# Values loaded by head onto 96 partitions, the first queries split off, and a new instruction order, in an attention and MLP kernel

## The chip, the cores and the metric

The kernel runs on one core of a Trainium2 chip. The core has TensorE (matrix products, PE in the profile; its weight loads are PEld), VectorE (DVE), ScalarE (ACT), GpSimd (POOL) and SyncE (SP). Each takes its own queue of instructions in order, and they meet through semaphores. Transfers between DRAM and the on-chip memory (SBUF, 128 partitions) run on 16 DMA engines. The metric is the device time of one execution in microseconds (us).

## The reference

Four batches of four heads, 1088 tokens each, head width 32. Attention is linear, over products of two sketches; its output goes through a layer with h - tanh(h).

```python
def phi(x):                                    # S1, S2: 8 x 32
    a = np.einsum('rd,bhsd->bhsr', S1, x)
    b = np.einsum('rd,bhsd->bhsr', S2, x)
    return np.einsum('bhsi,bhsj->bhsij', a, b).reshape(*x.shape[:-1], 64)
q_p, k_p = phi(q), phi(k)
kv = np.einsum('bhsf,bhsd->bhfd', k_p, v)
z = np.sum(k_p, axis=2)
num = np.einsum('bhsf,bhfd->bhsd', q_p, kv)
den = np.einsum('bhsf,bhf->bhs', q_p, z)[..., None] + 1e-06
x = (num / den)                                # as 4352 tokens x 128
h = x @ w_in                                   # 128 x 2048
out = (h - np.tanh(h)) @ w_out                 # 2048 x 128
```

## The kernel before

The program is a list of operations, each with an engine, what it reads and what it writes. A table, ORDER, gives each engine its queue by the operations' numbers, in the sequence in which they are created; a negative number n stands for -n dummy products on TensorE. Waits are derived from reads and writes. An operation at the head of its queue that waits holds everything behind it on that engine.

**Loads.** All large loads are issued by SP: load_k, load_v, load_q, load_w_in and load_w_out. Tokens of a batch are numbered 34 j + c with j from 0 to 31. Keys and queries of a batch come as 128 partitions (head, j) with 1088 numbers each (544 KB), batch 0's keys in two parts. Values sit in vx with 32 c + j as the partition, where c is one of four groups of 9, 9, 9 and 7 tokens; load_v issues one load for each group, onto 32 partitions, with all four heads (L432 to L439). A rule in load (L405) lets a load be issued only when the one that lies about 1.9 MB before it in the list has landed. Key, query and value buffers alternate between batches. Values are read by the products called sums; queries go through a transpose on VectorE (q_transpose, qT, L608), as keys do (kT, L567 and L710).

**Start.** Batch 0's keys are projected (kproj0), transposed (kab0), their products made (wk) and summed with the values (sums0). The first 256 queries have a path of their own (first_factors, first_numerators): qab, qd, qpd, qpdT; fold0 and the small copy swc0 (L726) on ScalarE, then qc, cd, dd, dden, drec, rT; then num0 and x0, which writes the first 256 tokens of xT. Weights are cast to bf16: w_in on ScalarE (casts, L819), w_out on GpSimd (L823).

**The layer.** Tokens are taken in groups: 128, 128, 256, then 512 at a time, 256 last. For a group, first_layer makes 16 blocks of h (L887) with a tanh on ScalarE after each 512 columns (L892); second_layer adds w_out products (L906) and a linear part (lin, L932) into one PSUM bank, which VectorE copies out (o, tile osb, L947) before the next group may start there; SP then stores it (L954). The linear part needs the product of the two weight matrices, kept as whi (ScalarE) and wlo (VectorE, L863). In the text h2, o1, lin0 and the like mean these operations of group 2, 1 and 0, and o#0 the copy out of group 0. The last group is stored with one DMA (L942):

```python
out=ob[B - 1, :, 26:34, :].rearrange("j (c z) e -> c j (z e)", z=2), in_=osb[u][:, 0:256]
```

**Later batches.** For batch b: key transpose kT, kproj, kab, gram, fold, wk on GpSimd, sums; query transpose qT, qproj, qf (L631), dt, den, rec, an, qp on GpSimd (L660), qpT, num (L680), and the casts into xT (L690).

Of the kernel before, what the change touches and what calls it, by code (L numbers as in the profile page):

```python
# [10 lines left out]
B, H, S, D = 4, 4, 1088, 32  # L11
# [5 lines left out]
OFF = (0, 9, 18, 27)  # L17
NT = 9
# [2 lines left out]

ORDER = {
    "tensor": (
# [17 lines left out]
    ),  # L41
    "scalar": (
# [9 lines left out]
    ),  # L52
    "vector": (
# [4 lines left out]
    ),  # L58
    "gpsimd": (
        21, 3, 22, 9, 7, 10, 8, 4, 23, 75, 82, 84, 59, 60, 134, 61, 62, 132, 150, 149, 151, 277, 302, 300, 280, 281,  # L60
        283, 285, 301, 431, 454, 456, 434, 435, 437, 439, 455, 579, 582, 583, 585, 587,
    ),
    "sync": (
# [4 lines left out]
    ),  # L68
}

# [256 lines left out]
def bass_polysketch_attn__then__act_tanh_shrink_kernel(nc, q, k, v, S1, S2, moe_w_in, moe_w_out, out):  # L327
# [28 lines left out]
    qraw = [sb(f"qraw{i}", [128, S]) for i in range(2)]  # L356
    kT = [sb(f"kT{i}", [128, 4 * NT * 32]) for i in range(2)]
    qT = [sb(f"qT{i}", [128, S]) for i in range(2)]
    vx = [sb(f"vx{i}", [128, H, NT, D]) for i in range(2)]
# [45 lines left out]
    def load(eng, key, sem, due, fn, nbytes, also=False, rate=300, name="load"):  # L405

        o = P.op(eng, nbytes / rate, fn, w=() if also else key if isinstance(key, list) else [key], sem=sem, due=due,
                 name=name)
        if also:
            P.also(o, key)  # L410
        if eng == "sync":
            ahead = nbytes
            for x, n in reversed(flow):
                ahead += n
                if ahead > AHEAD:
                    o.deps.add(x)
                    break
            flow.append((o, nbytes))
# [6 lines left out]
    def load_k(b, due):  # L425
        cuts = ((0, 512), (512, S)) if b == 0 else ((0, S),)
        for x, (lo, hi) in enumerate(cuts):
            load("sync", [("kraw", b % 2, y) for y in ((x,) if b == 0 else (0, 1))], f"k{b}{x}", due, lambda e, lo=lo, hi=hi: e.dma_start(  # L428
                out=kraw[b % 2][:, lo:hi], in_=k[b].rearrange("h (j c) d -> (h j) (c d)", j=32)[:, lo:hi]),
                512 * (hi - lo), rate=400 if b == 0 else 300, name=f"load k{b}")  # L430

    def load_v(b, due):  # L432
        src = v[b].rearrange("h (j c) d -> j h c d", j=32)
        for c in range(4):
            n = NT if c < 3 else 7
            load("sync", ("vx", b % 2), f"v{b}{c}", due + c, lambda e, c=c, n=n: e.dma_start(
                out=vx[b % 2][32 * c:32 * c + 32, :, 0:n, :].rearrange("j h t d -> j h (t d)"),
                in_=src[:, :, OFF[c]:OFF[c] + n, :].rearrange("j h t d -> j h (t d)")),
                128 * 128 * n, True, 226, name=f"load v{b}")  # L439

    def load_q(b, due):
        i = b % 2
        load("sync", ("qraw", i), f"q{b}", due, lambda e: e.dma_start(
            out=qraw[i][:, :], in_=q[b].rearrange("h (j c) d -> (h j) (c d)", j=32)), 512 * S, name=f"load q{b}")

    def load_w_in(x, due):
        load("sync", ("w_in_f", x), f"wi{x}", due, lambda e: e.dma_start(
            out=w_in_f[:, 512 * x:512 * x + 512], in_=moe_w_in[:, 512 * x:512 * x + 512]), 262144, rate=390, name="load w_in")

    def load_w_out(x, due):  # L450
        load("sync", ("w_out_f", x), f"wo{x}", due, lambda e: e.dma_start(
            out=w_out_f[:, 4 * x:4 * x + 4, :].rearrange("p z c -> p (z c)"),
            in_=moe_w_out[512 * x:512 * x + 512, :].rearrange("(ji z) c -> ji (z c)", z=4)), 262144, rate=390, name="load w_out")
# [152 lines left out]
    def q_transpose(b, part, lo, hi):  # L606
        i = b % 2
        P.op("vector", dve(hi - lo), lambda e: e.transpose(out=qT[i][:, lo:hi], in_=qraw[i][:, lo:hi]),  # L608
             r=[("qraw", i)], w=[("qT", i, y) for y in (range(2) if part is None else (part,))], name="qT")

    def layout(nblk):
        nb = (nblk + 3) // 4
# [347 lines left out]
    constants()  # L960
    load_s()
    load_k(0, 100)
    load_q(0, 150)
    load_v(0, 200)
    load_w_in(0, 400)
    load_w_in(1, 450)
    load_w_in(2, 500)
    load_w_in(3, 550)
    load_w_out(0, 650)
    load_w_out(1, 700)  # L970
    load_k(1, 750)
# [77 lines left out]
```

## Time and profile before

| | us |
|---|---|
| median of 3 runs | 110.84 |
| lowest and highest | 109.92, 111.91 |
| the profiled execution | 111.44 |
| its span in the profile | 109.7 |
| TensorE busy in it | 101.0 |
| ScalarE busy | 84.4 |
| VectorE busy | 46.5 |
| GpSimd busy | 41.8 |

The profile shows one execution. Its page gives each engine's busy time, the span in 40 equal slices with busy tenths, and the chain of work that ended last, followed back from the end. A row of a timeline reads: start, length, engine, line, operation, tile written and tile read, form, count, and in brackets how long the engine stood idle before and what released it. A row of a table of stretches reads: from and to, length, busy time and count of each engine, the granted TensorE clock, the mean busy share of the 16 DMA engines (counts can take it a little over 1), and GB/s. Matmuls overlap in the pipeline, so a busy TensorE is not TensorE at its peak. The granted clock was 0.998.

### The profile page before, as it was taken

What the parts mean: (1) busy time and instruction counts of PE and PEld (TensorE: products, weight loads), DVE (VectorE), ACT (ScalarE), POOL (GpSimd) and SP (SyncE); (2) the same over time, 40 slices, a digit from 0 to 9 for tenths busy, and PEclk for the clock granted to TensorE, in tenths of its full rate; (3) what the DMA queues carried; (4) which work ended last, traced back from release to release, by engine and by line L of the source; (5) the groups of instructions that cost most, each with busy time, mean ns of one, the idle gap of its engine ahead of it and who ended that gap; (6) DMA issues with size and microseconds to landing.
All of it is one profiled execution on the core that took longest, in us unless ns stands there. A gap on an engine that the chain in (4) does not pass through costs nothing.

```text
span 109.7 us, 3290 instructions
## 1 busy us (share of the span) xinstructions
PE 101.0 (92%) x1406; PEld 57.4 (52%) x1406; DVE 46.5 (42%) x88; ACT 84.4 (77%) x184; POOL 41.8 (38%) x46
## 2 busy tenths in 40 slices
PE   5999998898988989999999999999999999999940
PEld 4956677574646734443546543454444444345730
DVE  2737999736859384075017402527600200200210
ACT  3132479765964769798998979999979999999920
POOL 5204435799117998004999500269300000000000
PEclk9999999999999999999999999999999999999999
DMA  2999999996766821023000500410023041032061
GB/s 68 311 234 233 298 324 284 210 318 127 235 219 195 216 47 21 6 37 59 6 0 6 92 7 0 75 26 0 0 46 49 7 75 21 0 57 42 6 96 48
DMA packets 22195, 11.24 MB, mean 102 GB/s; under 512 B 17828, under 2 KB 20004, under 8 KB 22180
## 3 DMA queue, kind: packets, MB, share of 16 engines
q1 hardware_dynamic: 22100, 11.02, 40.9%
q8 instruction: 11, 0.18, 0.8%
q14 instruction: 4, 0.03, 0.1%
q10 hardware_dynamic: 80, 0.01, 0.1%
HBM read 8.79 MB, written 2.23 MB: 100 GB/s over the span
## 4 chain that ended last, share of the span: by engine, by line
PE 46%; DMA 32%; ACT 14%; DVE 2%; SPq 1%; issue 1%; DVEq 0%
PE ps L887 17%; PE ps L906 16%; DMA qraw<-in_q_dram 16%; ACT tt L892 13%; DMA w_out_f<-in_moe_w_out_dram 7%; DMA kraw<-in_k_dram 6%; PE ps L680 4%; DMA w_in_f<-in_moe_w_in_dram 4%; PE ps L932 2%; PE ps L585 2%; PE ps L913 1%; PE ps L624 1%; DVE qT L608 1%; ACT xT L690 1%; SPq L428 1%; PE ps L538 1%
## 5 line engine op out<-in xcount | busy, mean ns | idle before, releaser
L892 ACT ACTIVATE tt<-ps 128x512 bf16<-128x512 f32 x136 | 70.3, 659 | 4.8 <-PE ps L887 4.4
L887 PE MATMUL ps<-xT,w_in 128*128 128x512 bf16 (+2 forms) x176 | 48.1, 335 | 1.3 <-ACT w_inT L849 0.5
L906 PE MATMUL ps<-tt,w_out 128*128 128x512 bf16 (+2 forms) x160 | 41.3, 337 | 0.0
L887 PEld LDWEIGHTS ps<-xT,w_in 128*128 128x128 bf16 x176 | 17.5, 114 | 21.5 <-ACT tt L892 10.6
L947 DVE STREAM_TRANSPOSE osb<-ps 128x512 f32<-128x512 f32 (+2 forms) x10 | 5.9, 587 | 32.5 <-PE ps L906 32.5
L906 PEld LDWEIGHTS ps<-tt,w_out 128*128 128x128 bf16 x160 | 14.6, 99 | 9.1 <-ACT tt L892 0.7
L558 POOL TENSOR_TENSOR wk<-kab 128x768 f32<-128x768 f32 x10 | 15.1, 1508 | 8.9 <-DVE kab L530 8.3
L660 POOL TENSOR_TENSOR qp<-an,qf 128x768 f32<-128x768 f32 (+1 forms) x11 | 16.2, 1470 | 2.1 <-DVE an L651 1.3
L665 DVE STREAM_TRANSPOSE qpT<-qp 128x768 f32<-128x768 f32 (+1 forms) x12 | 11.1, 927 | 10.8 <-POOL qp L660 10.7
L637 POOL TENSOR_TENSOR dt<-qf 128x288 f32<-128x288 f32 x3 | 2.4, 796 | 16.8 <-DVE qf L631 16.8
L1020 PE MATMUL ps<-wz 128*128 128x128 bf16 x81 | 8.2, 256 | 0.0
L1020 PEld LDWEIGHTS ps<-wz 128*128 128x128 bf16 x81 | 6.4, 117 | 2.9 <-issue 2.6
L690 ACT CAST xT<-ps 128x256 bf16<-128x256 f32 (+3 forms) x16 | 5.3, 391 | 2.9 <-PE ps L680 2.9
L608 DVE STREAM_TRANSPOSE qT<-qraw 128x1088 f32<-128x1088 f32 (+2 forms) x5 | 5.4, 1072 | 3.0 <-DMA qraw<-in_q_dram 3.0
L680 PE MATMUL ps<-qpT,ndw 32*32 32x288 f32 (+1 forms) x256 | 6.2, 399 | 0.0
L631 DVE STREAM_TRANSPOSE qf<-ps 128x1152 f32<-128x1152 f32 (+1 forms) x4 | 5.2, 1307 | 0.8 <-PE ps L624 0.8
L567 DVE STREAM_TRANSPOSE kT<-kraw 128x1088 f32<-128x1088 f32 x3 | 3.9, 1297 | 2.1 <-DMA kraw<-in_k_dram 2.1
L680 PEld LDWEIGHTS ps<-qpT,ndw 32*32 32x32 f32 x256 | 3.2, 103 | 2.1 <-DVE qpT L665 0.6
L585 PEld LDWEIGHTS ps<-wk,vx 128*32 128x32 f32 x216 | 3.2, 110 | 1.9 <-issue 1.1
L530 DVE STREAM_TRANSPOSE kab<-ps 128x576 f32<-128x576 f32 (+2 forms) x5 | 3.1, 645 | 2.4 <-PE ps L522 2.4
L585 PE MATMUL ps<-wk,vx 128*32 128x64 f32 x216 | 4.1, 221 | 0.0
L538 PE MATMUL ps<-kab 128*64 128x32 f32 x72 | 3.1, 225 | 0.9 <-DVE kab L530 0.9
(97 smaller groups left out, 78.0 us busy)
## 6 DMA issues: line engine op xcount, KB each, us to landing
qraw<-in_q_dram SPq DMA_DIRECT2D x4, 544.0 KB, 5.9
vx<-in_v_dram SPq DMA_DIRECT2D x12, 144.0 KB, 6.7
kraw<-in_k_dram SPq DMA_DIRECT2D x3, 544.0 KB, 6.0
w_in_f<-in_moe_w_in_dram SPq DMA_DIRECT2D x4, 256.0 KB, 6.0
w_out_f<-in_moe_w_out_dram SPq DMA_DIRECT2D x4, 256.0 KB, 6.3
out_dram<-osb SPq DMA_DIRECT2D x16, 64.0 KB, 2.0
vx<-in_v_dram SPq DMA_DIRECT2D x4, 112.0 KB, 6.0
kraw<-in_k_dram SPq DMA_DIRECT2D x1, 288.0 KB, 3.2
```

The costliest lines, as they stand in the source:

```text
L558: P.op(eng, dve(64 * n) if eng == "vector" else pool(64 * n), lambda e: e.tensor_tensor(out=wk[i][:, t0:t1, :, :, :].rearrange("p t h i j ...
L585: ins = e.matmul(su[32 * h:32 * h + 32, 0:64], vx[b % 2][:, h, t, :], wk[i][:, t, h, :, :], start=(t == 0), stop=(t == NT - 1), tile_posit ...
L608: P.op("vector", dve(hi - lo), lambda e: e.transpose(out=qT[i][:, lo:hi], in_=qraw[i][:, lo:hi]), r=[("qraw", i)], w=[("qT", i, y) for y i ...
L660: e.tensor_tensor(out=qp[u][:, 4 * lo:4 * hi, :, :], in0=(pa if head else an[u][:, 4 * lo:4 * hi, :])[:, :, :, None].to_broadcast([128, m, ...
L665: P.op("vector", dve(64 * m), lambda e, lo=lo, hi=hi: e.transpose(out=qpT[u][:, :, 32 * lo:32 * hi].rearrange("p x (n j) -> p x n j", j=32 ...
L680: ins = e.matmul(ps[32 * h:32 * h + 32, c, 0:N], ndw[i][32 * c:32 * c + 32, y, 32 * h:32 * h + 32], qpT[u][32 * c:32 * c + 32, 2 * h + y, ...
L690: P.op("scalar", act(cols), lambda e: e.copy(dst, src), r=bank[c[0]:c[1]], w=[("x", (lo + 32 * first) // 32 + t) for t in range(cols // 32 ...
L887: ins = e.matmul(bk[:, n * y:n * y + n], w_tile(jb), xT[:, t0:t0 + n], start=True, stop=True)
L892: P.op("scalar", act(512), lambda e, ts=ts, bk=bk: e.activation(out=tt[:, ts, :], in_=bk, func=AF.Tanh, scale=-1.0), r=[kb], w=[("t", ts)] ...
L906: ins = e.matmul(acc[:, 0:n], w_out[:, jb, :], tt[:, ts, n * y:n * y + n], start=o.start and y == 0, stop=o.stop and y == per - 1)
L947: P.op("vector", dve(n), lambda e: e.transpose(out=osb[u][:, 0:n], in_=acc[:, 0:n]), r=[ka], w=[("osb", u, 0), ("osb", u, 1)], due=when(t0 ...
L1020: P.emit(lambda e: e.matmul(ps[:, 6, 0:128], wz[:, 0:128], wz[:, 0:128], start=True, stop=True))
```

## The change

Values are loaded one head at a time onto 96 partitions (groups 0 to 2), with a fifth load for group 3. Batch 0's queries are split into the first 256 columns, issued behind the keys, and the rest, issued behind w_in. The planner's rates are other numbers (they do not enter the program once ORDER is given). ORDER is replaced.

```diff
     def load_v(b, due):
-        src = v[b].rearrange("h (j c) d -> j h c d", j=32)
-        for c in range(4):
-            n = NT if c < 3 else 7
-            load("sync", ("vx", b % 2), f"v{b}{c}", due + c, lambda e, c=c, n=n: e.dma_start(
-                out=vx[b % 2][32 * c:32 * c + 32, :, 0:n, :].rearrange("j h t d -> j h (t d)"),
-                in_=src[:, :, OFF[c]:OFF[c] + n, :].rearrange("j h t d -> j h (t d)")),
-                128 * 128 * n, True, 226, name=f"load v{b}")
+        src = v[b].rearrange("h (j x) d -> h j x d", j=32)
+        for h in range(H):
+            load("sync", ("vx", b % 2), f"v{b}{h}", due + h, lambda e, h=h: e.dma_start(
+                out=vx[b % 2][0:96, h, :, :].rearrange("p t d -> p (t d)"),
+                in_=src[h, :, 0:27, :].rearrange("j (c t) d -> c j (t d)", c=3)),
+                96 * 1152, True, 370, name=f"load v{b}")
+        load("sync", ("vx", b % 2), f"v{b}4", due + 4, lambda e: e.dma_start(
+            out=vx[b % 2][96:128, :, 0:7, :].rearrange("j h t d -> j h (t d)"),
+            in_=src[:, :, 27:34, :].rearrange("h j t d -> j h (t d)")),
+            128 * 896, True, 300, name=f"load v{b}")
...
+    def load_q(b, due, part=None):
         i = b % 2
+        lo, hi = ((0, S), (0, 256), (256, S))[0 if part is None else part + 1]
+        load("sync", [("qraw", i, y) for y in (range(2) if part is None else (part,))], f"q{b}{part}", due, lambda e: e.dma_start(
+            out=qraw[i][:, lo:hi], in_=q[b].rearrange("h (j c) d -> (h j) (c d)", j=32)[:, lo:hi]), 512 * (hi - lo), rate=380,
...
     load_k(0, 100)
-    load_q(0, 150)
+    load_q(0, 150, 0)
     load_v(0, 200)
...
     load_w_in(3, 550)
+    load_q(0, 600, 1)
     load_w_out(0, 650)
```

q_transpose now reads the part of qraw that it transposes. With five new loads ahead of them, later operations have numbers 3 to 5 higher. Put back into names, ORDER differs in these places that matter here (b1, b2, b3 are the batches; qT(0) is the first 256 queries, qT(0') the rest):

| engine | before | after |
|---|---|---|
| SP, first loads | k0, q0, v0, w_in, w_out, k1, w_out, v1, q1, k2, v2, k3, q2, stores, q3, v3 among stores | k0, q0 first part, v0, w_in, q0 rest, w_out, k1, w_out, v1, q1, k2, v2, q2, k3, q3, 12 stores, v3 |
| ScalarE | ..., zs0, swc0, cast w_in, cast w_in, kvb x4, cast w_in, cast w_in, ndw0, tanh | ..., zs0, s2blk, cast w_in, swc0, cast w_in x3, kvb x4, tanh |
| VectorE, start | sbd, kab0, kab0, qT(0), wk, wk, qd, qT(0'), wk, cd, ..., kvd, drec, qf(0), rT, dt, x0, den, rT, rec, x0 | sbd, qT(0), kab0, kab0, qd, wk, wk, wk, qpdT, cd, ..., kvd, dden, qT(0'), drec, rT, rT, x0, qf(0), x0 |
| VectorE, later | ..., kab(b1), qpT, wlo, qT(b1), kT(b2), o#0, qf(b1), kT(b3), kab(b2), den, qT(b2), rec, o#1, ndw, qT(b3), o#2 | ..., kab(b1), qpT x3, kT(b2), wlo, qT(b1), qT(b2), o#0, qf(b1), kT(b3), o#1, qT(b3), kab(b2), den, rec, o#2 |
| GpSimd | wk, qpd x2, cast w_out x2, qp, cast w_out x2, qp | wk, qpd x2, cast w_out x4, qp, qp |
| TensorE | ..., kproj0, s2rep, gram0, qab, fold0, qc, sums0 x4, qproj, num0, spread, h0; ... num, lin0, h2 and qproj(b1), o1 | ..., kproj0, s2rep, qab, gram0, fold0, one sums0, qc, three sums0, num0, qproj, h0, spread; ... num, lin0, h2 and qproj(b1), o1 |

TensorE's dummy products go from 81 to 68.

More of the change, by code (lines that the diff above doesn't have):

```diff
@@ L23 @@
     "tensor": (
[17 rows of a table removed]
[17 rows of a table added]
     ),
     "scalar": (
[9 rows of a table removed]
[9 rows of a table added]
     ),
     "vector": (
[4 rows of a table removed]
[4 rows of a table added]
     ),
     "gpsimd": (
-        21, 3, 22, 9, 7, 10, 8, 4, 23, 75, 82, 84, 59, 60, 134, 61, 62, 132, 150, 149, 151, 277, 302, 300, 280, 281,
-        283, 285, 301, 431, 454, 456, 434, 435, 437, 439, 455, 579, 582, 583, 585, 587,
+        22, 3, 21, 9, 4, 7, 8, 10, 23, 78, 85, 87, 62, 63, 64, 65, 137, 135, 154, 153, 152, 281, 305, 284, 289, 285,
+        287, 306, 304, 436, 460, 439, 444, 440, 459, 442, 461, 584, 587, 590, 588, 592,
     ),
     "sync": (
[4 rows of a table removed]
[4 rows of a table added]
     ),
@@ L429, in load_k @@
                 out=kraw[b % 2][:, lo:hi], in_=k[b].rearrange("h (j c) d -> (h j) (c d)", j=32)[:, lo:hi]),
-                512 * (hi - lo), rate=400 if b == 0 else 300, name=f"load k{b}")
+                512 * (hi - lo), rate=400, name=f"load k{b}")
     def load_v(b, due):
-        src = v[b].rearrange("h (j c) d -> j h c d", j=32)
-        for c in range(4):
-            n = NT if c < 3 else 7
-            load("sync", ("vx", b % 2), f"v{b}{c}", due + c, lambda e, c=c, n=n: e.dma_start(
-                out=vx[b % 2][32 * c:32 * c + 32, :, 0:n, :].rearrange("j h t d -> j h (t d)"),
-                in_=src[:, :, OFF[c]:OFF[c] + n, :].rearrange("j h t d -> j h (t d)")),
-                128 * 128 * n, True, 226, name=f"load v{b}")
-    def load_q(b, due):
+        src = v[b].rearrange("h (j x) d -> h j x d", j=32)
[9 more added lines that the diff above has]
+    def load_q(b, due, part=None):
         i = b % 2
-        load("sync", ("qraw", i), f"q{b}", due, lambda e: e.dma_start(
-            out=qraw[i][:, :], in_=q[b].rearrange("h (j c) d -> (h j) (c d)", j=32)), 512 * S, name=f"load q{b}")
+        lo, hi = ((0, S), (0, 256), (256, S))[0 if part is None else part + 1]
+        load("sync", [("qraw", i, y) for y in (range(2) if part is None else (part,))], f"q{b}{part}", due, lambda e: e.dma_start(
+            out=qraw[i][:, lo:hi], in_=q[b].rearrange("h (j c) d -> (h j) (c d)", j=32)[:, lo:hi]), 512 * (hi - lo), rate=380,
+            name=f"load q{b}")
     def load_w_in(x, due):
@@ L608, in q_transpose @@
         P.op("vector", dve(hi - lo), lambda e: e.transpose(out=qT[i][:, lo:hi], in_=qraw[i][:, lo:hi]),
-             r=[("qraw", i)], w=[("qT", i, y) for y in (range(2) if part is None else (part,))], name="qT")
+             r=[("qraw", i, y) for y in (range(2) if part is None else (part,))], w=[("qT", i, y) for y in (range(2) if part is None else (part,))], name="qT")
     def layout(nblk):
```

68 rows, old and new, of the table ORDER are left out of this document.

## The prediction

> **What bounds the kernel now.** I read the page first, then the chain of waits, then stretches of time for the DMA, then the queues of the engines around the loads.
>
> ```profile
> span 109.7 us, 3290 instructions
> PE   5999998898988989999999999999999999999940
> DMA  2999999996766821023000500410023041032061
> PE 46%; DMA 32%; ACT 14%; DVE 2%; SPq 1%; issue 1%; DVEq 0%
> L892 ACT ACTIVATE tt<-ps 128x512 bf16<-128x512 f32 x136 | 70.3, 659 | 4.8 <-PE ps L887 4.4
> ```
>
> TensorE is nearly always busy from the second slice on, and a slice is 2.7 us. The DMA engines are full for the first nine slices, to about 25 us. The chain that ended last is DMA for a third of the span, and the next rows say where.
>
> ```profile
> 1.73 7.26 DMA qraw<-in_q_dram
> ...
> 20.88 6.10 DMA kraw<-in_k_dram
> ...
> 32.69 4.83 DMA qraw<-in_q_dram
> 37.52 0.02 issue
> 37.54 1.31 DVE qT L608
> 38.85 0.34 DVE osb L947
> 39.20 0.05 issue
> 39.24 0.60 PE ps L932 x2
> ```
>
> So until 37.5 us the loads pace the kernel, above all through VectorE, which takes its queue in order: the copy of the accumulator out of PSUM (osb, L947) stood behind a query transpose (L608) that waited for its load. From 39.2 us on TensorE, and for a stretch ScalarE, work without a gap that matters. Time lost ahead of 39 us is therefore lost at the end too.
>
> **How fast one transfer goes.** The next rows are stretches of time; the last two numbers are the mean busy share of the 16 DMA engines and GB/s.
>
> ```profile
> 8.00:9.00 1.00, 1.00 (x28) 0.90 (x24) 0.00 (x0) 0.66 (x4) 1.00 (x1) 1.00 1.08 214
> 12.00:13.00 1.00, 1.00 (x73) 1.00 (x72) 1.00 (x3) 0.97 (x2) 0.39 (x1) 1.00 0.98 361
> 30.00:31.00 1.00, 1.00 (x40) 0.46 (x40) 0.00 (x0) 0.82 (x2) 0.67 (x1) 1.00 1.03 418
> 36.50:37.00 0.50, 0.50 (x6) 0.38 (x4) 0.00 (x0) 0.44 (x1) 0.39 (x1) 1.00 0.83 287
> 108.00:108.50 0.50, 0.00 (x0) 0.00 (x0) 0.00 (x0) 0.00 (x0) 0.00 (x0) 1.00 0.27 96
> 109.00:109.65 0.65, 0.00 (x0) 0.00 (x0) 0.00 (x0) 0.00 (x0) 0.00 (x0) 0.74 0.00 0
> ...
> vx<-in_v_dram SPq DMA_DIRECT2D x12, 144.0 KB, 6.7
> out_dram<-osb SPq DMA_DIRECT2D x1, 128.0 KB
> ```
>
> GB/s over (16 x share) is the rate of one busy engine: 361/15.7 = 23.0 with weights, 418/16.5 = 25.4 at best, 287/13.3 = 21.6 with values, but 214/17.3 = 12.4 while the first values arrive on 32 partitions. The row at 108 us is the one to stop at. Nothing but the last store is running, 128 KB in 128 pieces of 1 KB, and it has 0.27 of the engines, about 4 of 16, at 96/4.3 = 22.2 each. Its DRAM side is written as 4 x 32 x 256 (L942: column group outermost), its SBUF side as 128 rows. The outermost size, 4, is the number of engines that it got. The old values loads have 32 outermost on both sides, and the DMA is full while they run.
>
> **The change part by part.** *The values.* Four loads of 128 KB (144 KB for 9 token groups) and a narrower one become four loads of one head (96 partitions, 110,592 bytes) and a tail. The bytes and the runs of 1,152 bytes stay. But the DRAM side of a head load is now 3 x 32 x 288, with the token group outermost, against 96 rows of SBUF. By the last store's row that gives 3 engines, not 16. The tail has 32 outermost on both sides, as the old loads have: 16 engines. Each of the three engines then carries 4 x 36.9 = 147 KB of head loads a batch. At 22.5 GB/s (between 21.6 and 23.0) that is 6.6 us; by 25.4 it is 5.8. The old loads took 557 KB / 214 to 287 = 1.9 to 2.6 us.
>
> The page "DMA: Bandwidth & Descriptors" of the Trainium skill, section "Why a DMA increments its semaphore by 16 and not by 1", says that the number of engines is the largest one up to 16 that divides the outermost size of both patterns. By that rule the store gets 4 (the trace agrees, 0.27 of 16) and a head load 3; no run here shows a head load.
>
> Every other load is spread over all 16 engines and is complete only when its share on those three is. So the three engines' queue sets every landing. Up to and with the queries of batch 2 each of them carries, in KB: three batches of keys 104, three of queries 104, all weights 131, three batches of values 442, tails 22: 803. At 22.5 GB/s: 35.7 us. Data start at about 1.8 us (the DMA row has two tenths of the first slice), and a landing is seen some 0.6 us after the last byte (the store: its bytes end before 109.0, the span at 109.7). Queries of batch 2 land at 38.1 us. In the same way keys of batch 2 (614 KB ahead) land at 29.7, keys of batch 1 (357) at 18.3, the first values (198) at 11.2, the first weights (214) at 11.9.
>
> *The first 256 queries ahead.* The rows are VectorE's and ScalarE's timelines.
>
> ```profile
> 9.01 0.45 DVE L608 STREAM_TRANSPOSE qT<-qraw 128x256 f32<-128x256 f32 x1 [1.09 <-DMA qraw<-in_q_dram]
> 14.13 1.12 DVE L631 STREAM_TRANSPOSE qf<-ps 128x896 f32<-128x896 f32 x1 [0.15 <-PE ps L624]
> 10.55 0.17 ACT L726 COPY sw<-ps 128x8 f32<-128x8 f32 x1 [1.12 <-PE ps L547]
> 11.75 1.26 ACT L819 CAST w_in<-w_in_f 128x512 bf16<-128x512 f32 x2 [1.04 <-DMA w_in_f<-in_moe_w_in_dram]
> 16.74 2.56 ACT L892 ACTIVATE tt<-ps 128x512 bf16<-128x512 f32 x5
> ```
>
> These queries now come before the values, so the 1.09 us that VectorE waited go. The new order also puts qf (1.12) behind the first x0. Against it, ScalarE's queue now has the first w_in cast ahead of the copy swc0 (L726). Under the forecast that cast waits for weights until 11.9, takes 0.63, and swc0 comes at 12.5 where it was at 10.55; the product qc on TensorE waits for it, and behind qc stand sums, numerators and the first h0. With the rest of the queries (290 KB ahead, 15.3) and their transpose in front of the denominators, the first tanh comes at about 18, not 16.7. This and the gain alike are swallowed by the next wait, so I price them at nothing; without that wait they are +1.2.
>
> *The new order.* These rows are VectorE's and TensorE's timelines between 24 and 40 us.
>
> ```profile
> 24.89 0.29 DVE L863 TENSOR_TENSOR wlo<-ps,whi 128x128 bf16<-128x128 f32 x1 [1.52 <-ACT whi L862]
> 25.09 1.30 DVE L608 STREAM_TRANSPOSE qT<-qraw 128x1088 f32<-128x1088 f32 x1
> 27.01 1.31 DVE L567 STREAM_TRANSPOSE kT<-kraw 128x1088 f32<-128x1088 f32 x1 [0.61 <-DMA kraw<-in_k_dram]
> 28.25 0.28 DVE L947 STREAM_TRANSPOSE osb<-ps 128x128 f32<-128x128 f32 x1
> 28.58 0.40 PE L906 MATMUL ps<-tt,w_out 128*128 128x128 bf16 x4
> 33.35 0.77 PE L538 MATMUL ps<-kab 128*64 128x32 f32 x18 [0.90 <-DVE kab L530]
> 39.24 0.39 PE L932 MATMUL ps<-xT,whi 128*128 128x512 bf16 x1 [0.43 <-DVE osb L947]
> ```
>
> On VectorE, batch 2's key transpose now stands ahead of wlo, and batch 2's query transpose ahead of the first copy out (o#0). TensorE's linear part (lin0) needs wlo, and its second accumulation group (o1) needs o#0; behind each stands everything else of TensorE. So keys at 29.7 + 1.31 + 0.29 hold lin0 to 31.3, where wlo was there at 25.2 before. Then come five h2 products and qproj; then queries at 38.1 + 1.31 + 0.28 hold o1 to 39.7, where it began at 28.58, with the same five h2 done: 11.1 us late. Of that, the gaps that TensorE had before between 28.6 and 39.3 come back, 0.90 + 0.43 = 1.3, since the work is all there by then: 9.8 net. Past that point VectorE and GpSimd repeat the old chain (qf, dt, den, an, qp, num) as much later, beside TensorE's h3 and o3, and nothing catches up.
>
> Small edits: five more DMA issues at about 0.4 us each, on SP, hidden by its waits; two w_out casts ahead of two qp products on GpSimd, hidden by the wait for keys; 13 fewer dummy matmuls, in gaps; batch 3's values behind twelve stores, needed some 30 us later; changed rates only name costs to the planner, which doesn't run. If the wait of 38.1 is gone, these are worth half a microsecond either way.
>
> The sum: span 109.7 + 9.8 = 119.5. The profiled execution took 111.44, 0.60 over the median 110.84 and 1.74 over its span. On the median: 110.84 + 9.8 = 120.6; I say 120.5.
>
> **The rivals.** *All 16 engines.* If the engines were counted on the written side alone (96 rows), the store's 4 would hold and the loads would be wide. Then the three-engine queue vanishes, and the values' 12.4 GB/s an engine may rise to the others' 23. The gain is at most 1.09 + 1.12 at the start and 1.3 in TensorE's gaps, 3.5: 107.3; with half of it 109. I take 108. What speaks for it: 8-9 us is slow with 32 partitions written. The page "SBUF — State Buffer", section "Door 1: The DMA port swizzle (why [64,N] ≈ [32,N])", says that partitions 0 to 31 reach half of the 16 ports, as the halved rate would have it. Against it: the store's SBUF side had 128 rows, and that did not help.
>
> *Three engines, but quick.* At 25.4 GB/s, the queries land at 1.8 + 31.6 + 0.6 = 34.0, 4.1 earlier: 116.5. At 20 they land at 42.6: 125.
>
> *Three engines, slow pieces.* If values keep 12.4 GB/s per engine, 442 KB alone take 35.6: the queries land near 54 and the kernel takes some 136. The row at 36.5 us (21.6) speaks against it.
>
> *Caught up later.* If TensorE does other work in the wait, as little as 3 to 4 us may remain: 114. Its queue being in order speaks against it.
>
> **How the numbers follow.** Three engines at 116.5 to 125: 0.76. All 16: 0.11 (half over 2% faster). Caught up: 0.08, mostly over 2% slower. Slow pieces: 0.05. The range 115 to 125.5 holds the first and some of the third, 0.8. About 2% is what a measurement of this kernel can tell. Faster 0.06, same 0.06, slower 0.88.
>
> **What would show it.** Stretches with a DMA share near 0.2 between 5 and 36 us with about 70 GB/s; values landing 6 us or more after their first byte; VectorE waiting some 5 us for qraw ahead of 39 us with osb right behind; TensorE idle near 26 to 31 and 33 to 39. If the share stays near 1.0 while values load, the forecast is wrong at its first step.

## The result, and the profile after

| | before | after |
|---|---|---|
| median, us | 111.29 (4 runs) | 124.94 (4 runs) |
| lowest and highest | 109.92, 111.91 | 124.05, 125.43 |
| the profiled execution | 111.44 | 125.43 |
| its span | 109.7 | 123.7 |
| granted TensorE clock | 0.998 | 0.909 |

The changed kernel takes 1.131 times as long, interval 1.116 to 1.146: slower by 13.7 us, where the forecast was 120.5 in a range of 115 to 125.5. The table holds every execution; the ratio, and the medians and ratios below, leave out executions in a second, slower state (two of the four of before here, without which the difference is 14.6 us), and each ratio is against runs of the kernel before on the same chip.

The page of the changed kernel first: its span, TensorE's busy tenths, the granted clock in tenths, the DMA share in tenths, and the shares of the chain that ended last.

```profile
span 123.7 us, 3259 instructions
PE   5990699997450889999999999999999999999950
PEclk9999558999855559999999999999999999999996
DMA  3489685951962610113340032003102304022042
PE 53%; ACT 16%; DMA 13%; SPq 10%; DVE 2%; issue 2%; DVEq 0%
```

A slice is 3.1 us. The DMA engines are full (a 9) in three of the first twelve slices, where before they were so in eight of the first nine. TensorE has two holes, around 11 and around 38 us, and at each the clock row shows fives: the mean clock of before, 0.998, leaves no room for them. The chain now holds 10% of SP's queue (the issue of the values' loads) beside the DMA.

VectorE's timeline, a row being start, length, line, operation, tile written and tile read:

```profile
30.65 1.31 DVE L572 STREAM_TRANSPOSE kT<-kraw 128x1088 f32<-128x1088 f32 x1 [2.60 <-DMA kraw<-in_k_dram]
31.89 0.25 DVE L868 TENSOR_TENSOR wlo<-ps,whi 128x128 bf16<-128x128 f32 x1
...
39.06 1.31 DVE L613 STREAM_TRANSPOSE qT<-qraw 128x1088 f32<-128x1088 f32 x1 [5.71 <-DMA qraw<-in_q_dram]
40.30 0.27 DVE L952 STREAM_TRANSPOSE osb<-ps 128x128 f32<-128x128 f32 x1
```

TensorE's, at the three places where it waits for these and for the first values:

```profile
13.45 0.66 PE L744 MATMUL ps<-wk,vx 128*32 128x64 f32 x16 [3.90 <-DMA vx<-in_v_dram]
...
32.20 0.23 PE L937 MATMUL ps<-xT,wlo 128*128 128x128 bf16 x1 [2.17 <-DVE wlo L868]
...
40.63 0.61 PE L911 MATMUL ps<-tt,w_out 128*128 128x128 bf16 x4 [4.88 <-DVE osb L952]
```

And stretches of time (the last three numbers are the granted clock, the DMA share and GB/s):

```profile
28.00:29.00 1.00, 1.00 (x43) 0.79 (x41) 0.05 (x1) 0.27 (x1) 0.92 (x2) 1.00 0.19 78
33.00:34.00 1.00, 0.66 (x20) 0.32 (x32) 0.35 (x1) 1.00 (x3) 0.00 (x0) 0.50 1.04 366
37.00:38.00 1.00, 0.00 (x0) 0.00 (x0) 0.00 (x0) 0.00 (x0) 0.00 (x0) 0.50 0.21 83
42.00:43.00 1.00, 1.00 (x10) 0.88 (x9) 1.00 (x1) 0.32 (x2) 0.70 (x1) 0.50 0.43 71
47.00:48.00 1.00, 1.00 (x12) 0.91 (x10) 0.25 (x1) 0.00 (x0) 1.00 (x1) 1.00 0.00 0
```

At 28 us only head loads are moving, on 0.19 of 16 engines: three. At 37 us 0.21 are busy, three again, with what is left of them and of the wide loads' pieces behind them. The queries of batch 2 land at 39.06, VectorE has waited 5.71 for them, and the first copy out (osb) comes right behind their transpose. TensorE's second accumulation group, o1, can start only then, at 40.63: 12.05 later than the 28.58 of before. But the whole span is 14.0 longer. So 2.0 more are lost behind o1, with all the work there, and the last two rows say what is different behind it: in the stretch from 42 us TensorE, busy in all of it, has half its clock, and only in the one from 47 us all of it.

### The profile page after: what moved, and what is told of

Its sections match the earlier page's. It is cut to its first block, busy times and chain, and to the rows that moved or that the text cites. A ratio compares the mean times of both kernels' runs of the same rounds, so it can differ in the third digit from the quotient of the medians.

```text
span 123.7 us, 3259 instructions
## 1 busy us (share of the span) xinstructions
PE 104.2 (84%) x1380; PEld 59.5 (48%) x1393; DVE 48.0 (39%) x88; ACT 84.1 (68%) x184; POOL 41.8 (34%) x46
## 4 chain that ended last, share of the span: by engine, by line
PE 53%; ACT 16%; DMA 13%; SPq 10%; DVE 2%; issue 2%; DVEq 0%
PE ps L892 17%; PE ps L911 16%; ACT tt L897 15%; SPq L435 7%; DMA qraw<-in_q_dram 7%; DMA vx<-in_v_dram 6%; PE ps L685 4%; PE ps L937 2%; PE ps L1026 2%; PE ps L744 2%; PE ps L629 2%; PE ps L918 2%; SPq L439 2%; PE ps L527 1%; PE ps L590 1%
## 5 line engine op out<-in xcount | busy, mean ns | idle before, releaser
L892 PE MATMUL ps<-xT,w_in 128*128 128x512 bf16 (+2 forms) x170 | 46.6, 342 | 0.9 <-issue 0.4
L911 PEld LDWEIGHTS ps<-tt,w_out 128*128 128x128 bf16 x160 | 15.5, 105 | 15.7 <-DVE osb L952 5.4
L670 DVE STREAM_TRANSPOSE qpT<-qp 128x768 f32<-128x768 f32 (+1 forms) x12 | 10.9, 920 | 7.3 <-POOL qp L665 7.3
L824 ACT CAST w_in<-w_in_f 128x512 bf16<-128x512 f32 x4 | 2.5, 618 | 4.9 <-DMA w_in_f<-in_moe_w_in_dram 4.8
L744 PE MATMUL ps<-wk,vx 128*32 128x64 f32 x72 | 2.4, 314 | 3.9 <-DMA vx<-in_v_dram 3.9
L828 POOL CAST w_out<-w_out_f 128x512 bf16<-128x512 f32 x4 | 2.4, 612 | 8.9 <-DMA w_out_f<-in_moe_w_out_dram 8.7
L937 PE MATMUL ps<-xT,wlo 128*128 128x512 bf16 (+2 forms) x10 | 3.5, 347 | 2.2 <-DVE wlo L868 2.2
```

Source lines behind the costliest of these rows:

```text
L670: P.op("vector", dve(64 * m), lambda e, lo=lo, hi=hi: e.transpose(out=qpT[u][:, :, 32 * lo:32 * hi].rearrange("p x (n j) -> p x n j", j=32 ...
L892: ins = e.matmul(bk[:, n * y:n * y + n], w_tile(jb), xT[:, t0:t0 + n], start=True, stop=True)
L911: ins = e.matmul(acc[:, 0:n], w_out[:, jb, :], tt[:, ts, n * y:n * y + n], start=o.start and y == 0, stop=o.stop and y == per - 1)
L937: P.op("tensor", 3 + n / 2.4, lambda e, o, x=x: e.matmul(acc[:, 0:n], x[:, :], xT[:, t0:t0 + n], start=o.start, stop=o.stop), r=[(nm,)] + ...
```

## The experiments

The questions are: is it the width of the loads (theory), or the new order alone; is it the place of the transposes in VectorE's queue that turns a late load into lost time; what are the other 2 us; and which load is the one that counts. Four runs make a square of the two main edits, and the rest take one step each. Operations are called as in the sections on the kernel and the change.

**1. Wide value loads in the new order.** Everything of the change stays, but the five values loads of a batch have 32 rows outermost on both sides.

```diff
-        src = v[b].rearrange("h (j x) d -> h j x d", j=32)
-        for h in range(H):
-            load(... out=vx[b % 2][0:96, h, :, :] ...
+        src = v[b].rearrange("h (j c) d -> j h c d", j=32)
+        for x, (c, n, lo, hi) in enumerate(((0, NT, 0, 4), (1, NT, 0, 4), (2, NT, 0, 2), (2, NT, 2, 4), (3, 7, 0, 4))):
+            load(... out=vx[b % 2][32 * c:32 * c + 32, lo:hi, 0:n, :] ...
```

> Changed kernel, with its order, its split queries and its five values loads a batch kept, but each values load written with the 32 rows j outermost on both sides (two token groups whole, one in two halves by heads, one narrow). Theory (three busy engines per head load delay every landing): DMA share near 1.0 while values load, queries of batch 2 land before 30 us, TensorE idles no more than 1 us at a time after 16 us, the granted clock stays at 1.0, time 106 to 111. Rival (the new order of VectorE's queue, with batch 2's transposes ahead of the copies out, is what costs): 118 to 124.

Measured: 112.98 us, ratio 1.012 (1.004 to 1.020). One stretch of this kernel, and then rows of VectorE's and TensorE's timelines:

```profile
28.00:29.00 1.00, 0.58 (x10) 0.34 (x15) 0.70 (x1) 0.97 (x3) 0.00 (x0) 1.00 0.95 387
```

```profile
29.56 1.31 DVE L608 STREAM_TRANSPOSE qT<-qraw 128x1088 f32<-128x1088 f32 x1 [0.86 <-DMA qraw<-in_q_dram]
...
31.13 0.40 PE L906 MATMUL ps<-tt,w_out 128*128 128x128 bf16 x4 [0.80 <-DVE osb L947]
```

The DMA share goes from 0.19 to 0.95 in the same stretch, the queries land 9.5 us earlier, o1 starts 9.5 earlier, and 12.0 us of the 13.7 are gone. Without the narrow loads nearly all of the loss is gone. What is left, 1.2%, fits the new order: o1 still waits for the copy out behind a transpose, 2.55 later than before, so the order is no gain even with fast loads. The time expected, no longer than that of before, did not come.

**2. Head loads in the old order.** The kernel before, with load_v of the change and nothing else; queries in one load.

```diff
-        for c in range(4):
-            load(... out=vx[b % 2][32 * c:32 * c + 32, :, 0:n, :] ...
+        for h in range(H):
+            load(... out=vx[b % 2][0:96, h, :, :] ...
+        load(... out=vx[b % 2][96:128, :, 0:7, :] ...
```

> Kernel before, with its order and its undivided queries, and only the values loaded by head onto 96 partitions (the fifth load issued right behind the fourth). Theory: DMA share near 0.2 for long stretches, queries of batch 2 land near 39 us as in the changed kernel; the old order has o#0 ahead of that wait but o#1 behind it, so TensorE is late by 5 to 7 us, with half clock after the waits: time 115 to 120. Rival (order): 110 to 112.

Measured: 121.1 us, ratio 1.089 (1.078 to 1.101), 1 us above the range expected. A row of VectorE's timeline and one of TensorE's:

```profile
39.83 1.31 DVE L570 STREAM_TRANSPOSE kT<-kraw 128x1088 f32<-128x1088 f32 x1 [5.64 <-DMA kraw<-in_k_dram]
...
41.86 1.27 PE L541 MATMUL ps<-kab 128*64 128x32 f32 x18 [5.00 <-DVE kab L533]
```

The old order pays too, but at another load than expected: here SP issues the keys of batch 3 behind the head loads of batch 2, VectorE waits 5.64 for those, and TensorE waits 5.00 for kab, which stands behind their transpose. It was not the queries of batch 2 with o#1 behind them.

**3. Another VectorE queue.** The change with all its narrow loads, but the transposes of batch 2 and 3 behind the copies out that need no load (wlo, qT(b1), o#0, qf, kT(b2), o#1, kab, den, rec, o#2, qT(b2), kT(b3)).

```diff
-  138, 136, 297, 174, 161, 313,
-  193, 280, 452, 204, 462, 299, 282, 283, 219, 290, 286, 288, 296, 274,
+  138, 136, 174, 161, 193, 280,
+  297, 204, 299, 282, 283, 219, 313, 452, 290, 286, 288, 296, 462, 274,
```

> Changed kernel with its loads; only VectorE's queue is other: wlo, the query transpose of batch 1, o#0, qf(b1), then the key transpose of batch 2, o#1, kab, den, rec, o#2, and only then the query transpose of batch 2 and the key transpose of batch 3. Theory (late landings reach TensorE through VectorE's queue): landings stay as late (share near 0.2, queries of batch 2 near 39 us), but o1 starts before 34 us and TensorE's wait of 4.9 us goes: time 115 to 119. Rival (the landings hold the kernel wherever VectorE waits, through the next consumer): 122 to 126.

Measured: 114.49 us, ratio 1.028 (1.021 to 1.036). VectorE's timeline, and then one stretch:

```profile
30.71 0.27 DVE L952 STREAM_TRANSPOSE osb<-ps 128x128 f32<-128x128 f32 x1
...
39.68 1.31 DVE L613 STREAM_TRANSPOSE qT<-qraw 128x1088 f32<-128x1088 f32 x1 [1.00 <-DMA qraw<-in_q_dram]
```

```profile
28.00:29.00 1.00, 1.00 (x64) 0.61 (x45) 0.29 (x1) 0.20 (x1) 0.92 (x2) 1.00 0.19 78
```

The loads are as narrow (0.19) and the queries land as late (39.68), and still 10.4 of the 13.7 us are gone: the copy out comes at 30.71 instead of 40.30, and VectorE waits only 1.00. A late load costs little in itself here (2.8% over before is left, start included); it costs what stands behind the instruction that waits for it. The gain is larger than expected.

**4. The clock kept up.** The change with 180 more dummy products for TensorE, put where it waits: 60 ahead of the first sums, 35 and 85 in two blocks of h2, which were moved ahead of the waiting products.

```diff
-  76, -1, 99,
+  76, -1, -60, 99,
...
+                for _ in range({(2, 0): 35, (2, 7): 85}.get((g, jp), 0)):
+                    e.matmul(bk[:, 0:128], wz[:, 0:128], wz[:, 0:128], start=True, stop=True)
```

> Changed kernel with 180 more dummy products on TensorE: 60 ahead of the first sums0, 35 and 85 in the two waits after 30 us (written into the PSUM bank of an h2 block that is moved ahead of the wait and overwrites them). Theory (the waits of TensorE cost a second time, by the half clock that follows them): granted clock 0.98 or more in the mean, landings and o1 as late as before (40 to 41 us), time 121 to 123.5. Rival (the half clock falls on work that other waits hide): 124.5 to 125.5.

Measured: 122.5 us, ratio 1.098 (1.091 to 1.106). The span of its profiled execution is 120.7. One stretch in the wait, and then o1 on TensorE's timeline:

```profile
37.00:38.00 1.00, 1.00 (x22) 1.00 (x20) 0.00 (x0) 0.00 (x0) 0.00 (x0) 1.00 0.20 78
```

```profile
40.91 0.84 PE L913 MATMUL ps<-tt,w_out 128*128 128x128 bf16 x12 [0.99 <-DVE osb L954]
```

The loads stay narrow (0.20) and o1 starts as late, at 40.91, but the clock stays at 1.00 and the kernel is 2.4 us faster by the medians, 3.0 by the profiled executions. This kernel follows the forecast's own sum: o1 is 12.33 late, the span is 11.0 longer, and 1.3 came back. One of the two moved blocks now runs ahead of o1; its two products of h2 take 0.43 us at half clock in the changed kernel, so the move itself can account for no more than that of the 3.0. The rest of the loss behind o1 in the changed kernel is the clock.

**5. Both mends.** Experiment 1 with the queue of experiment 3.

```diff
-            load(... out=vx[b % 2][0:96, h, :, :] ...
+            load(... out=vx[b % 2][32 * c:32 * c + 32, lo:hi, 0:n, :] ...
-  138, 136, 297, 174, 161, 313, 193, 280, 452,
+  138, 136, 174, 161, 193, 280, 297, 204, 299,
```

> Both earlier mends at once: values loads with 32 rows outermost on both sides, and VectorE's queue with wlo and the copies out ahead of batch 2's and 3's transposes; the split queries and the rest of the new order stay. If the two costs are separate, VectorE waits for no load after 20 us, o1 starts near 28.5 us as before: 109 to 111. If the new order has a cost of its own on the other engines: 112 to 114.

Measured: 110.56 us, ratio 1.004 (0.997 to 1.011): the time of before. That completes the square:

| us | queue of the change | queue of experiment 3 |
|---|---|---|
| head loads | 124.94 | 114.49 |
| wide loads | 112.98 | 110.56 |

Mending the loads alone brings 12.0, mending the queue alone 10.4, both 14.4; by the ratios, since experiment 5 ran on another chip than 1 and 3, it is 11.9, 10.3 and 12.7 points of 13.1. The two don't add up, because each takes away the same wait: the late load needs the queue to do harm, and the queue needs the late load.

**6. The queries of batch 2 ahead of the values of batch 2**, in SP's list; the loads stay narrow.

```diff
-  155, 156, 157, 158, 159, 160, 162, 307,
+  155, 162, 156, 157, 158, 159, 160, 307,
```

> Changed kernel with one DMA issue moved: SP issues batch 2's queries ahead of batch 2's five values loads. Theory (what holds these queries is the 147 KB a head-loaded batch that stands ahead of them in the three engines' queues): they land 6 to 7 us earlier, near 32.5 us, o1 near 34 us, TensorE's clock stays up after it: 115 to 119. Rival (a shortage of total bandwidth or of SP's issue time): they land at 37 us or later, 123 to 126.

Measured: 125.39 us, ratio 1.136 (1.125 to 1.147): nothing gained, where 6 us or more were expected. Two rows of VectorE's timeline and one of TensorE's:

```profile
34.16 0.28 DVE L952 STREAM_TRANSPOSE osb<-ps 128x128 f32<-128x128 f32 x1
...
41.76 1.31 DVE L572 STREAM_TRANSPOSE kT<-kraw 128x1088 f32<-128x1088 f32 x1 [5.53 <-DMA kraw<-in_k_dram]
...
43.32 1.04 PE L911 MATMUL ps<-tt,w_out 128*128 128x256 bf16 x4 [5.12 <-DVE osb L952]
```

The first copy out comes 6.1 earlier, as it should. The next load in line, the keys of batch 3, is behind the same values now; VectorE waits 5.53 for it, and the second copy out stands behind that. The wait moved by one load and kept its length.

**7. Two groups instead of three in a head load**; the third group is loaded like the fourth, 32 rows outermost. Each of the engines in use then still carries 4 x 64 x 1,152 / 2 = 147 KB a batch, as in the change, but the head loads hold a third less.

```diff
-                out=vx[b % 2][0:96, h, :, :].rearrange("p t d -> p (t d)"),
-                in_=src[h, :, 0:27, :].rearrange("j (c t) d -> c j (t d)", c=3)),
+                out=vx[b % 2][0:64, h, :, :].rearrange("p t d -> p (t d)"),
+                in_=src[h, :, 0:18, :].rearrange("j (c t) d -> c j (t d)", c=2)),
```

> Changed kernel with head loads of two token groups (64 rows, outermost size 2 on the DRAM side) and the third group loaded as 32 rows with all heads. A third of the head loads' bytes now goes over 16 engines, but each of two engines still carries 147 KB a batch. Theory (the most loaded engine's queue sets every landing): queries of batch 2 land at 38.5 to 41 us, each engine carrying 9 KB a batch more, time 124 to 127. Rival (it is the rate of the head loads as a whole, so a third fewer bytes in them helps): queries land by 34 us, 116 to 120. If the number of engines were not the outermost size, the time would be near 113.

Measured: 127.26 us, ratio 1.155 (1.142 to 1.167). One stretch, and then VectorE's timeline:

```profile
30.00:31.00 1.00, 0.67 (x32) 0.18 (x10) 0.00 (x0) 0.45 (x2) 1.00 (x1) 1.00 0.13 52
```

```profile
41.48 1.31 DVE L614 STREAM_TRANSPOSE qT<-qraw 128x1088 f32<-128x1088 f32 x1 [6.19 <-DMA qraw<-in_q_dram]
```

0.13 is two engines of 16, at 26 GB/s each, as with three (78 / 3). With 3 outermost there are three engines, with 2 two, with the 4 of the last store four. The most loaded engine sets the landing, not the bytes: with less in the narrow loads, and the same on each of their engines, the queries come 2.4 later, not earlier. That is a little past the 41 us expected: the 9 KB more a batch on each engine, 28 KB by then, are 1.2 us at 22.5 GB/s, and the other 1.2 stay unexplained.

**8. Only the first queries split off**, in the kernel before, the rest right behind batch 0's values.

```diff
-    load_q(0, 150)
+    load_q(0, 150, 0)
...
+    load_q(0, 250, 1)
```

> Kernel before, with only batch 0's queries split: the first 256 columns ahead of the values, the rest right behind them; everything else in the old order. VectorE's wait of 1.09 us for the first part goes; the second part may be waited for in its place. If the start gains and nothing is late behind it: 109.5 to 111 where before is 111 to 112. If the wait moves to the second part: no change, within 1 us.

Measured: 110.50 us, ratio 1.001 (0.994 to 1.008). A row of VectorE's timeline, one of TensorE's and one of ScalarE's:

```profile
7.13 0.40 DVE L610 STREAM_TRANSPOSE qT<-qraw 128x256 f32<-128x256 f32 x1
...
14.48 0.60 PE L626 MATMUL ps<-qT,sw 32*32 32x224 f32 x12 [1.50 <-issue]
...
17.88 2.56 ACT L894 ACTIVATE tt<-ps 128x512 bf16<-128x512 f32 x5
```

No change that can be measured, though the wait did not move to the second part: the 1.09 are gone, and VectorE waits for no load in their place. But TensorE then pauses 1.50 inside the projection of the queries with no wait in the profile, and the first tanh is at 17.88, where before it was at 16.74. What the split is worth without that pause is not shown.

**9. Queries of batch 2, keys and queries of batch 3 all ahead of the values of batch 2.**

```diff
-  155, 156, 157, 158, 159, 160, 162, 307, 314,
+  155, 162, 307, 314, 156, 157, 158, 159, 160,
```

> Changed kernel with SP issuing the queries of batch 2 and the keys and queries of batch 3 all ahead of batch 2's values. With only batch 2's queries moved, o#0 came 6 us earlier and the time did not: VectorE then waited 5.5 us for batch 3's keys, which stood behind the same values. Theory (three engines' queue in the order of issue): now no load that VectorE waits for is behind these values, o1 starts near 35 us and o2 near 38 us: 115 to 119. If values of batch 2 are then late for their own sums, or SP's wait for a landing holds the rest: 121 or more.

Measured: 117.2 us, ratio 1.060 (1.053 to 1.067). VectorE's timeline at the first copy out, TensorE's at o1, and VectorE's next transpose:

```profile
33.79 0.28 DVE L952 STREAM_TRANSPOSE osb<-ps 128x128 f32<-128x128 f32 x1
...
34.87 0.63 PE L911 MATMUL ps<-tt,w_out 128*128 128x128 bf16 x4
35.60 1.27 DVE L572 STREAM_TRANSPOSE kT<-kraw 128x1088 f32<-128x1088 f32 x1
```

With the next two loads moved as well, the gain that experiment 6 missed is there, 7.7 us, and kT(b3) follows without a long wait. That settles why that one gained nothing. Some 6% over before remain; the values of batches 0 and 1 are still ahead of these loads, and that they are the rest was not tried by itself.

**10. Two queues for the first values.** In the kernel before, ScalarE issues the loads of groups 2 and 3 of batch 0. It asks whether the 12.4 GB/s per engine that the forecast read there comes of loading 32 partitions at a time.

```diff
-            load("sync", ("vx", b % 2), f"v{b}{c}", due + c, ...
+            load("scalar" if b == 0 and c > 1 else "sync", ("vx", b % 2), f"v{b}{c}", due + c, ...
```

> Kernel before with the last two values loads of batch 0 (partitions 64 to 127) issued by ScalarE, so that they run beside SP's two (partitions 0 to 63). If 32 partitions at a time are what slows the values (12.4 GB/s an engine), GB/s between 5 and 9 us rises from 214 to 248 to 300 or more and the first weights land 1 us earlier: 109.5 to 111. If the slow rate is that of 1,152 byte pieces: the same GB/s and time as before.

Measured: 111.04 us, ratio 1.003 (0.998 to 1.008). Two stretches:

```profile
8.00:9.00 1.00, 0.81 (x19) 0.63 (x19) 0.00 (x0) 0.28 (x2) 0.94 (x1) 1.00 1.02 256
...
10.00:11.00 1.00, 0.58 (x9) 0.17 (x9) 1.00 (x3) 0.00 (x0) 0.00 (x0) 1.00 1.03 213
```

256 GB/s instead of 214 at 8 us, but 213 two stretches later, where before had 238: still some 13 to 16 GB/s an engine. Inconclusive on what holds that rate down, and no gain in time. The 214 is also the slowest of the stretches of before from 5 to 11 us; the others have 217 to 248, 14 to 19 GB/s an engine.

**11. Batch 0's values wide, the others by head.**

```diff
+        if b == 0:
+            src = v[b].rearrange("h (j c) d -> j h c d", j=32)
+            for x, (c, n, lo, hi) in enumerate(((0, NT, 0, 4), (1, NT, 0, 4), (2, NT, 0, 2), (2, NT, 2, 4), (3, 7, 0, 4))):
...
+            return
```

> Changed kernel with batch 0's values alone loaded with 32 rows outermost on both sides; batches 1 to 3 by head. By the queue's sum each of the three engines has 120 KB less ahead of every later load, 5.3 us at 22.5 GB/s: first tanh near 17 us, queries of batch 2 land at 33 to 35 us, time 118 to 121. If batch 0's values are hidden by other waits: 123 or more. If they were all that matters: 113 to 115.

Measured: 121.4 us, ratio 1.095 (1.088 to 1.102). The first tanh of the changed kernel, on ScalarE's timeline, to compare with:

```profile
21.39 1.57 ACT L897 ACTIVATE tt<-ps 128x512 bf16<-128x512 f32 x3 [2.58 <-PE ps L892]
```

And of this kernel the first tanh, and the transpose of batch 2's queries on VectorE's timeline:

```profile
16.21 1.57 ACT L905 ACTIVATE tt<-ps 128x512 bf16<-128x512 f32 x3 [2.31 <-PE ps L900]
...
36.05 1.31 DVE L621 STREAM_TRANSPOSE qT<-qraw 128x1088 f32<-128x1088 f32 x1 [5.50 <-DMA qraw<-in_q_dram]
```

The start is as early as before (first tanh 16.21; in the change 21.39), and the queries are 3.0 earlier than in the change. The time is 3.5 lower, by the queries and not by the start's 5.2: an earlier start is swallowed by the wait that follows, as the forecast said. The queue's sum was off here: it had the queries 5.3 earlier, at 33 to 35 us, and the time at 118 to 121. One reason may be that the wide loads of batch 0 are slow themselves, 229 GB/s at shares of 0.92 and 1.02 from 5 to 7 us, 14 to 16 GB/s an engine where the sum took 22.5; that was not tried by itself.

**12. An earlier first layer.** Experiment 5 with the rest of batch 0's queries ahead of w_in, and x0 and the first blocks of h ahead of their transpose and projection.

```diff
-  32, 33, 34, 35, 36, 37, 38, 39,
+  32, 33, 38, 34, 35, 36, 37, 39,
```

> A version meant to be faster than both: wide values loads, copies out ahead of the later transposes (110.9 before), the rest of batch 0's queries issued ahead of w_in, and x0 and the first three h0 ahead of that rest's transpose and projection. If the start is what is left to gain, the first tanh comes at 15 to 15.7 us in place of 16.7: 109 to 110.5. If TensorE's gap of 1.4 us in num0 that no wait explains stays, no gain: 110.5 to 112.

Measured: 112.75 us, ratio 1.021 (1.015 to 1.026): slower than experiment 5. ScalarE's timeline, and a row of TensorE's:

```profile
15.77 1.53 ACT L892 ACTIVATE tt<-ps 128x512 bf16<-128x512 f32 x3
19.15 0.37 ACT L811 COPY ndw<-ps 128x256 f32<-128x256 f32 x1 [1.85 <-PE ps L808]
19.42 0.60 ACT L892 ACTIVATE tt<-ps 128x512 bf16<-128x512 f32 x1
...
18.45 0.67 PE L808 MATMUL ps<-kvb,e 128*128 128x256 f32 x2 [1.44 <-DVE qf L631]
```

The first tanh is 1.0 ahead of that of before, and the fourth stands behind the copy ndw, which waits 1.85 for the product called spread (L808). That one waits 1.44 for VectorE's qf, which comes behind the transpose and the projection that were put back: the gain is given back within 4 us. A version that beats both kernels was not found.

## Why the prediction came out as it did

*The engines of a head load: right.* The forecast of three engines from the last store's row is seen in the change (0.19 at 28 us), and with 2 outermost in experiment 7 there are two (0.13). The rival that the loads would be wide falls with that. The rule of the Trainium skill that the forecast set beside it ("DMA: Bandwidth & Descriptors", "Why a DMA increments its semaphore by 16 and not by 1") gives 3, 2 and 4 for the three cases, and the traces agree with all of them.

*The queue of the three engines: right in kind, 0.9 us short.* The queries of batch 2 landed at 39.06 (forecast 38.1), the keys at 30.65 (29.7). The first values were 2 us off. SP's timeline of the changed kernel shows the issues, and a row of its chain that ended last the landing:

```profile
2.22 3.20 SPq L435 DMA_DIRECT2D vx<-in_v_dram  x4
...
21.99 6.75 SPq L435 DMA_DIRECT2D vx<-in_v_dram  x4
```

```profile
5.46 7.85 DMA vx<-in_v_dram
```

The first values landed at 5.46 + 7.85 = 13.3, forecast 11.2: 198 KB in 13.3 - 0.6 - 1.8 = 10.9 us is 18 GB/s an engine while the other thirteen work, not 22.5; alone it was 26. And the four issues of batch 2 held SP for 6.75 us, where the forecast had 0.4 each, "hidden by its waits". The chain passes through them, and with the issues at the start they are most of its 10% of SP; no run takes them away. By the trace they need not have delayed the landing: the share is 0.19 to 0.21 from 27 to 31 us, ahead of the queries' issue at 30.76, and again from 36 to 39, so the three engines had work on both sides of it.

*VectorE's queue, in order, with wlo and the first copy out behind the transposes: right.* Experiment 3 takes this step alone away and 10.4 us go with it. That the work would be caught up later, a rival at 114, falls: TensorE has nothing else to do in the wait.

*"The gaps ... 1.3 come back ... 9.8 net": the step that failed.* From o1 on the forecast let everything run as before, less the gaps of 1.3. In the change 2.0 were lost instead, a swing of 3.3 us, since the waits of 3.90, 2.17 and 4.88 on TensorE were followed by stretches at half clock (0.50 from 33 to past 42, 1.00 at 47). Experiment 4 keeps the clock, has o1 as late, and gets the 1.3 back. With the 0.9 of the landing this is the whole difference between the forecast span, 119.5, and the measured 123.7: 0.9 + 3.3 = 4.2. Four stretches of the changed kernel say when the clock changed:

```profile
12.00:13.00 1.00, 0.00 (x0) 0.00 (x0) 0.00 (x0) 0.00 (x0) 0.00 (x0) 0.70 0.60 161
...
19.00:20.00 1.00, 1.00 (x57) 0.96 (x51) 0.39 (x2) 0.00 (x0) 0.02 (x1) 0.89 0.54 207
...
32.00:33.00 1.00, 0.80 (x7) 0.62 (x7) 1.00 (x2) 0.32 (x1) 0.00 (x1) 0.94 0.99 266
...
46.00:47.00 1.00, 1.00 (x9) 0.77 (x8) 0.97 (x3) 0.60 (x1) 0.45 (x1) 0.73 0.21 33
```

The stretch ahead of each is at one clock throughout and the one behind it at the other, so these means put the falls to one half at 12.40 and 32.88 and the returns at 19.22 and 46.54. The half clock behind o1, from 40.63 to 46.54, is worth some 3.0 of the 3.3 us, an estimate from these figures: half of 5.9. The four changes lie 6.8, 13.7 and 13.7 us apart: two, four and four times 3.41. The page "TensorE: Matmul & The Clock Gate" of the Trainium skill, section "Part 1: The HAM clock gate", says that the clock is halved after an idle window of some 3.4 us and given back after a busy one, and that the window is free-running. The traces agree: the spacing is that of whole windows, and the profiled executions of experiments 1 and 3, without the long waits, have a mean clock of 1.0. They also show that an idle window need not be idle throughout: in the one that ends at 32.88, TensorE stood still for 2.17 of the 3.41. The forecast listed TensorE's idle time as its sign and did not ask what the idle time does to the clock behind it.

*The start at nothing: right for the change, and only for it.* Its size was off: the first tanh came at 21.39, not at about 18, behind values that were 2.1 late and a half clock from 12.40 to 19.22; the wait that follows swallowed this too. Experiment 11 gives the start back and gains no more than its earlier queries explain. Where the big wait is gone it counts, as the forecast's condition had it: experiment 3, whose first values come by head, stays 2.8% above before, and experiment 5, with wide ones, does not. Batch 0's loads were not widened alone in that queue, so this fits but isn't shown.

## What to carry to other kernels

Write a load so that its outermost size on both sides spreads over all engines (here 32 rows and not 3 groups); a narrow load delayed the wide ones behind it here, because a wide one is complete only when its piece on the busiest engine is. Then look at what stands behind the instruction that waits for a load: moving one load or one transpose is of use only when the next one in the queue isn't behind the same transfer. And price a wait of several us on TensorE twice, once for itself and once for the half clock behind it (here 3.3 us, behind waits of 2.17 and 4.88).

## What the hardware showed that was not expected

The half clock lasted beyond the end of the wait: TensorE was busy again from 40.63 and still had 0.50 in the stretch at 42, up to 46.54. Filling the waits with 180 useless products, with two blocks of h2 moved for it, was worth 2.4 us of 124.9.

SP was held while issuing: four loads took 6.75 us where the same four at the start took 3.20. Toward their end only the three engines are busy (0.21 and 0.19 of 16 in the stretches at 27 and 28 us); that the queues of these three hold SP up was not tried by itself.

In experiment 1, with wide loads, TensorE paused inside the numerators with nothing in the profile that it waited for. Its timeline:

```profile
14.95 0.31 PE L793 MATMUL ps<-qpdT,kvd 32*32 32x128 f32 x3 [1.39 <-issue]
```

Its first tanh was no earlier than before (16.76 and 16.74), and experiment 8 has such a pause of 1.50; why the issue paused stays open. So does the rate while the first values arrive on 32 partitions, 12.4 to 19 GB/s an engine before and 13 to 19 from two queues.
